# A hand-ordered two-stage chunk pipeline for a linear-attention and spectral-filter kernel

What was changed: the per-chunk attention output is formed in its natural layout and then transposed, the bonus term is summed on VectorE in place of TensorE, the key product moves to GpSimd, the inverse transform is done at half length, all small PSUM tiles share one ring of six buffers, and the order of all instructions is written by hand in place of the automatic one.

## Chip, cores and metric

One core of one Trainium2 chip. The metric is device microseconds of one execution of the program. The engines are named as the profile names them: PE (TensorE, matmul), PEld (its weight load), DVE (VectorE), ACT (ScalarE), POOL (GpSimd), SP (SyncE, which only issues DMA transfers here). With one core only the time itself can tell a slow execution. Executions of the same kernel differ by 1 to 2%, so I quote medians and, where there is one, the ratio with its 95% interval.

The device time of an execution is a little longer than the span of its profile: the profiled run of the kernel before took 224.11 us on the device with a span of 222.3 us. All the positions in a trace below are in the span's time.

## The reference

Batch 4, 8 heads, 768 steps, head size 48, model width 384. Stage 1 is a recurrent attention with a per-step decay, stage 2 a long convolution by FFT between two gates.

```python
def _attn_ref(r, k, v, w, u):                # all [4, 8, 768, 48], u [8, 48]
    state = zeros((B, H, D, D))
    for t in range(S):
        cur = einsum('bhd,bhe->bhde', u[None] * kt, vt)      # the bonus term
        y[:, :, t] = einsum('bhd,bhde->bhe', rt, state + cur)
        state = wt[..., None] * state + einsum('bhd,bhe->bhde', kt, vt)
    return y

def _moe_ref(x, w_proj, filter_fft, w_out):  # x = y as [4, 768, 384]
    proj = x @ w_proj
    x1, x2, x3 = ...                         # three slices of 384 columns
    X2 = rfft(x2, axis=1);  H = rfft(filter_fft, axis=0)
    x2_conv = irfft(X2 * H, n=S, axis=1)
    return (x1 * x2_conv * x3) @ w_out
```

## The kernel before

The recurrence is done in chunks of 128 steps, 24 chunks in all (4 batches of 6). A chunk needs the cumulated decay (two matmuls against triangular masks), exponentials of it, keys and queries scaled by them, scores masked to the past, and a carried state. When a batch's six chunks are done, its [384 x 768] transposed output `xT` feeds stage 2: projections, sums and differences of halves, a forward transform by matmul, spectral products on DVE, an inverse transform by matmul, a gate multiply, the output projection. Stage 2 of one batch is filled in between the chunks of the next. The parts that matter here:

```python
    psA = ctx.enter_context(tc.tile_pool(name="psA", bufs=3, space=PSUM))
    psS = ... bufs=1;  psT = ... bufs=1;  psB = ... bufs=2      # 8 banks in four pools
    ...
    def part_a(idx):
        ...
        nc.gpsimd.tensor_copy(out=v_heads(v_bufs[idx % NV]), in_=lv)
        nc.gpsimd.tensor_mul(rk[:, :, 0:D], rb[:, :, 0:D], lk)          # r*k, for the bonus
        nc.vector.tensor_mul(kh[:, :, 0:D], lk, csi)                    # scaled key, on DVE
        ...
    def part_b(idx):
        for x, o in ((kh, 0), (rk, HP)):                                # 8 transposes on PE
            for j in range(HP):
                nc.tensor.transpose(tk[:, o + j, :], x[:, 2 * j:2 * j + 2, :], ident)
        nc.scalar.activation(out=tkT, in_=tk, func=AF.Copy)             # 128 x 1024
        ...
        for j in range(HP):                                             # bonus: 4 matmuls
            nc.tensor.matmul(kv[:, C + 2 * j:C + 2 * j + 2], tkT[:, HP + j, :], u_sb[:, j, :], ...)
        ...                                                             # scores sc, mask mt
        nc.vector.tensor_copy(out=cc, in_=kv[:, C:])
        nc.gpsimd.tensor_mul(vc, v_heads(vb), cc.to_broadcast([L, H, D]))
        ...                                                             # state
    def part_c(idx, xT):        # output straight in transposed layout: 19 matmuls of 128 columns
        for cb in range(CB):
            ...
            for n, (lh, rh) in enumerate(ops):
                nc.tensor.matmul(yT[:, cb, :], lh, rh, ...)
        nc.scalar.activation(out=xT[:, :, ci * L:(ci + 1) * L], in_=yT, func=AF.Copy)
    ...
        def prods():            # six DVE instructions over 3 x 384 columns, bf16
            nc.vector.tensor_mul(ua, xr, HR);  nc.vector.tensor_mul(ub, xi, HI)
            nc.vector.tensor_sub(pr, ua, ub)
            nc.vector.tensor_mul(ua, xr, HI);  nc.vector.tensor_mul(ub, xi, HG)
            nc.vector.tensor_add(pi, ua, ub)

        def inv(cb, hf):        # six of these per batch: 6 matmuls of 384 columns each
            for n, q in enumerate((0, 2, 4, 1, 3, 5)):
                m = m2n[:, q - 2, :] if (hf and q >= 2) else m2[:, q, :]
                nc.tensor.matmul(ps, z(f"P{q % 2}")[:, q // 2, cb * L:(cb + 1) * L], m, ...)
            nc.vector.tensor_mul(z("y")[:, cb, sl], ps, z("g")[:, cb, sl])
    ...
    for idx in range(len(chunks) + 1):      # automatic order over this program
        part_a(idx); load_weights(idx); issue_loads(idx + 3)
        fill(3)                             # three waiting pieces of stage 2
        part_c(idx - 1, ...)
        fill(3)
        part_b(idx)
        fill(3)
```

## Time and profile before

Median 222.61 us of three runs (221.51 to 223.82) at the time of the prediction; 223.22 us of four beside the kernel after.

| profiled run, span 222.3 us | PE | DVE | ACT | POOL |
|---|---|---|---|---|
| busy, whole span (us) | 181.1 | 143.8 | 124.1 | 81.6 |
| busy in one batch period of 46.4 us | 41.6 | 32.3 | 28.2 | 18.1 |

The view by stretches gives one whole batch period, from one batch's first spectral product to the next. Columns: stretch and length, then busy time with the count of instructions for PE, PEld, DVE, ACT and POOL, then the granted clock, the DMA share and GB/s.

```profile
66.90:113.28 46.38, 41.57 (x438) 28.80 (x436) 32.32 (x54) 28.22 (x55) 18.06 (x27) 1.00 0.65 134
```

PE is busy 41.57 of 46.38 us at full clock.

The groups of DVE instructions by shape show something else that the argument needs. Columns: line, engine, operation, output and inputs, shapes, count, then busy us and mean ns of one, then idle time before.

```profile
L456 DVE TENSOR_TENSOR sd_1437<-xT_841 128x384 bf16<-128x384 bf16 x3 | 3.4, 1127 | 1.7 <-ACT xT_841 L403 1.7
...
L456 DVE TENSOR_TENSOR sd_2907<-xT_2325 128x384 bf16<-128x384 bf16 x3 | 1.6, 521 | 2.7 <-ACT xT_2325 L403 2.7
L477 DVE TENSOR_TENSOR U_1007<-X_906,HI 128x1152 bf16<-128x1152 bf16 x1 | 1.4, 1440 | 0.0
...
L457 DVE TENSOR_TENSOR sd_1439<-xT_841 128x384 bf16<-128x384 bf16 x3 | 1.0, 346 | 0.0
...
L477 DVE TENSOR_TENSOR U_3119<-X_3083,HI 128x1152 bf16<-128x1152 bf16 x1 | 0.7, 749 | 0.0
```

The same instruction, bf16 from SBUF to SBUF, has two prices. The sum of two xT slices (L456) takes 1,127 ns in mid-kernel and 521 ns in the last batch (358, 847 and 359 ns; at the last of them POOL has run out of work); and the product at L477 1,440 ns and, with POOL idle, 749 ns. The difference of the same slices (L457), which follows each sum, takes 346 ns. The six products of a batch together take 5.5 us in mid-kernel (0.76 + 1.09 + 0.76 + 1.44 + 0.75 + 0.74, from the same view) and 4.5 us in the last batch.

### The profile page before, as it was taken

The numbers are of one execution on the slowest core, as the hardware profiler recorded it, in microseconds if no ns is written. First come the engines' busy times: TensorE is split into PE (matmuls) and PEld (weight loads), VectorE is DVE, ScalarE is ACT, GpSimd is POOL, SyncE is SP. The second block draws the span as 40 slices with busy tenths as digits, with TensorE's granted clock in tenths as the row PEclk, the third lists the DMA queues.
The fourth block names the chain that finished last, engine by engine and source line by source line (L and its number), as shares of the span: only waits on it lengthen the run. The fifth ranks groups of instructions, "written<-read, shape, count | busy, mean of one in ns | idle before, by whom it ended". The sixth has DMA issues, their size and how long they took to land.

```text
span 222.3 us, 4668 instructions
## 1 busy us (share of the span) xinstructions
PE 181.1 (81%) x1778; PEld 123.3 (55%) x1778; DVE 143.8 (65%) x260; ACT 124.1 (56%) x233; POOL 81.6 (37%) x129
## 2 busy tenths in 40 slices
PE   0066797988798999978898999887979999779882
PEld 0054555766555657666465666665656666645341
DVE  8946366387759845776679384786696537734730
ACT  2396447467676346576773445767842475656022
POOL 8740366447312433463423235363232432400000
PEclk9999559699999999999999999999999999999998
DMA  6999999939598244995950709987401041000022
GB/s 132 175 307 229 282 166 193 182 66 198 108 192 158 56 85 100 257 179 112 174 108 2 143 19 278 173 170 137 79 3 35 0 147 69 4 0 0 3 106 108
DMA packets 105863, 27.44 MB, mean 123 GB/s; under 512 B 100464, under 2 KB 105456, under 8 KB 105840
## 3 DMA queue, kind: packets, MB, share of 16 engines
q1 hardware_dynamic: 105040, 25.96, 54.7%
q0 software_dynamic: 800, 1.18, 3.1%
q8 instruction: 14, 0.23, 0.5%
q14 instruction: 9, 0.07, 0.1%
HBM read 23.59 MB, written 4.72 MB: 127 GB/s over the span
## 4 chain that ended last, share of the span: by engine, by line
PE 53%; DVE 20%; ACT 12%; DMA 6%; issue 6%; SPq 1%; POOL 1%; DVEq 0%; ACTq 0%; POOLq 0%
PE yT L400 10%; PE ps_p L431 9%; PE ps_i L485 9%; DMA r_84<-in_r_dram 5%; PE ps_o L495 4%; DVE mt L362 4%; PE ps_f L254 3%; PE rT L317 3%; PE ps_f L246 3%; PE sc L355 3%; DVE g L443 2%; ACT tkT L337 2%; DVE sd_1437 L456 2%; DVE sd_2179 L456 2%; DVE sd_695 L456 2%
## 5 line engine op out<-in xcount | busy, mean ns | idle before, releaser
L362 DVE TENSOR_TENSOR mt<-sc,mask_excl 128x1024 bf16<-128x1024 f32 x24 | 29.2, 1216 | 1.1 <-PE sc L355 1.1
L337 ACT ACTIVATE tkT<-tk 128x1024 bf16<-128x1024 bf16 x24 | 24.6, 1023 | 1.4 <-PE tk L335 1.2
L490 DVE TENSOR_TENSOR y<-ps_i,g 128x384 bf16<-128x384 f32 x24 | 12.8, 555 | 16.5 <-PE ps_i L485 16.5
L431 PEld LDWEIGHTS <-wproj 128*128 128x128 bf16 x144 | 13.4, 99 | 14.1 <-issue 6.9
L499 ACT ACTIVATE o<-ps_o 128x384 f32<-128x384 f32 x24 | 11.4, 493 | 15.8 <-PE ps_o L495 15.8
L318 ACT ACTIVATE csi<-csi 128x384 f32<-128x384 f32 x24 | 11.6, 482 | 13.8 <-PE csi L310 13.8
L360 DVE COPY cc<-kv 128x8 f32<-128x8 f32 x24 | 3.9, 164 | 23.0 <-PE kv L347 22.8
L400 PE MATMUL yT<-ident,vc 128*128 128x128 bf16 x72 | 16.2, 225 | 2.2 <-POOL vc L364 2.2
L495 PE MATMUL ps_o<-wout,y 128*128 128x384 bf16 x72 | 15.2, 326 | 1.3 <-DVE y L490 0.7
L364 POOL TENSOR_TENSOR vc<-v_87,cc 128x384 bf16<-128x384 bf16 x8 | 6.6, 830 | 16.3 <-DVE cc L360 16.2
L272 PE MATMUL m2t<-ident,F 128*128 128x128 bf16 x18 | 2.8, 305 | 11.5 <-DVE ident L190 11.5
L324 DVE TENSOR_TENSOR qT<-rT,e_96 128x512 bf16<-128x512 f32 x12 | 8.2, 687 | 5.0 <-ACT e_96 L319 5.0
L355 PE MATMUL sc<-qT,tkT 48*128 48x128 bf16 x192 | 11.3, 223 | 0.0
L321 POOL TENSOR_TENSOR rk_93<-r_84,ld_k 128x384 bf16<-128x384 f32 x6 | 6.0, 999 | 13.1 <-PE tk L335 7.0
L400 PE MATMUL yT<-qT,st_98 128*128 128x128 bf16 x72 | 9.9, 219 | 0.7 <-DVE kh_91 L322 0.6
L368 POOL TENSOR_TENSOR phi<-e_95,blk 128x8 f32<-128x8 f32 x12 | 2.9, 244 | 20.4 <-ACT e_95 L319 17.3
L495 PEld LDWEIGHTS <-y 128*128 128x128 bf16 x72 | 6.6, 97 | 6.7 <-DVE y L490 1.9
L254 PE MATMUL ps_f<-ab,F 128*128 128x384 bf16 x48 | 9.7, 327 | 0.2
L400 PE MATMUL yT<-mt,v_87 128*128 128x128 bf16 x80 | 8.9, 219 | 1.1 <-DVE mt L362 1.1
L364 POOL TENSOR_TENSOR vc<-v_86,cc 128x384 bf16<-128x384 bf16 x8 | 6.6, 831 | 8.2 <-DVE cc L360 8.2
L400 PE MATMUL yT<-mt,v_88 128*128 128x128 bf16 x80 | 8.7, 225 | 0.8 <-DVE mt L362 0.8
L324 DVE TENSOR_TENSOR qT<-rT,e_95 128x512 bf16<-128x512 f32 x12 | 8.2, 684 | 1.4 <-ACT e_95 L319 1.2
(278 smaller groups left out, 538.4 us busy)
## 6 DMA issues: line engine op xcount, KB each, us to landing
ld_w<-in_w_dram SPq DMA_DIRECT2D x24, 192.0 KB, 3.9
ld_k<-in_k_dram SPq DMA_DIRECT2D x24, 192.0 KB, 3.2
ld_v<-in_v_dram SPq DMA_DIRECT2D x24, 192.0 KB, 4.2
out_dram<-o SPq DMA_DIRECT2D x3, 1152.0 KB, 5.2
filt<-in_moe_filter_fft_dram SPq DMA_DIRECT2D x2, 1152.0 KB, 8.2
r_82<-in_r_dram SPq DMA_DIRECT2D x6, 192.0 KB, 4.0
r_83<-in_r_dram SPq DMA_DIRECT2D x6, 192.0 KB, 3.6
r_84<-in_r_dram SPq DMA_DIRECT2D x6, 192.0 KB, 4.0
```

The lines of the kernel that those rows point to most:

```text
L254: nc.tensor.matmul(ps, F[:, ti, c0:c0 + L], x[:, ti, :], start=(ti == 0), stop=(ti == NT - 1),)
L324: nc.vector.tensor_mul(qT, rT, e[:, :, 0:L])
L337: nc.scalar.activation(out=tkT, in_=tk, func=AF.Copy)
L355: nc.tensor.matmul(sc[:, par, j, :], tkT[p0:p0 + D, j, :], qT[p0:p0 + D, j, :], start=True, stop=True,)
L362: nc.vector.tensor_mul(mt, sc.rearrange("p q j t -> p (q j) t"), _mid(mask_excl, H))
L364: nc.gpsimd.tensor_mul(vc, v_heads(vb), cc.to_broadcast([L, H, D]))
L400: nc.tensor.matmul(yT[:, cb, :], lh, rh, start=(n == 0), stop=(n == len(ops) - 1))
L431: nc.tensor.matmul(ps, wproj[:, cb, col0:col0 + L], xT[:, cb, sl], start=(cb == 0), stop=(cb == CB - 1),)
L456: nc.vector.tensor_add(z(f"sd{0}")[:, :, sl], lo, hi)
L485: nc.tensor.matmul(ps, z(f"P{q % 2}")[:, q // 2, cb * L:(cb + 1) * L], m, start=(n == 0), stop=(n == 5),)
L490: nc.vector.tensor_mul(z("y")[:, cb, sl], ps, z("g")[:, cb, sl])
L495: nc.tensor.matmul(ps, z("y")[:, cb, ti * L:(ti + 1) * L], wout[:, cb, :], start=(cb == 0), stop=(cb == CB - 1),)
```

## The change

Its intent is to take work from PE and to fill the idle POOL, and to let a batch period shrink from PE's pace to one that all engines share. The core of the diff, with cuts:

```diff
-    psA = ctx.enter_context(tc.tile_pool(name="psA", bufs=3, space=PSUM))
+    psA = ctx.enter_context(tc.tile_pool(name="psA", bufs=6, space=PSUM))
-    psT = ...
-    psB = ...
[...]
+    u_bc = consts.tile([L, H, D], FP32)          # u on all partitions
[...]
+    def bonus_a(idx):
+        nc.gpsimd.tensor_mul(rk, r_bufs[idx % NR][:, :, 0:D], t["lk"])
+        nc.gpsimd.tensor_mul(t["rku"], rk, u_bc)
+        nc.gpsimd.tensor_copy(out=t["vb"], in_=t["lv"])
+    def bonus_b(idx):
+        nc.vector.tensor_reduce(out=cc, in_=t["rku"], axis=AX.X, op=ALU.add)
+        nc.gpsimd.tensor_mul(t["vc"], t["vb"], cc.to_broadcast([L, H, D]))
[...]
-        nc.vector.tensor_mul(kh[:, :, 0:D], lk, csi)
+        nc.scalar.activation(out=en, in_=csi, func=AF.Exp, scale=-1.0)
+        nc.gpsimd.tensor_mul(kh[:, :, 0:D], t["lk"], en)
[...]
-        for x, o in ((kh, 0), (rk, HP)):
-            for j in range(HP):
-                nc.tensor.transpose(tk[:, o + j, :], x[:, 2 * j:2 * j + 2, :], ident)
+        for j in range(HP):
+            nc.tensor.transpose(tk[:, j, :], kh[:, 2 * j:2 * j + 2, :], ident)
[...]
+            nxt = s1.tile([L, HP, 2, D], BF16, tag="S", name="S")      # state: added on PE,
+            nc.vector.tensor_mul(nxt, kv, t["phi"].to_broadcast(...))   # scaled on DVE
[...]
-    def part_c(idx, xT):          # 19 matmuls of 128 columns, transposed layout
+    def output(idx):              # natural layout: 1 of 384, 4 of 96, 8 of 48 columns
+        nc.tensor.matmul(y, ident, t["vc"], start=True, stop=False)
+        ... 4 x qT against S; 8 x mt against vb
+        nc.scalar.activation(out=xn, in_=y, func=AF.Copy)
+    def turn_x(idx, xT):          # three transposes and a second eviction
+        for cb in range(CB):
+            nc.tensor.transpose(yt[:, cb, :], t["xn"][:, cb * L:(cb + 1) * L], ident)
+        nc.scalar.activation(out=xT[:, :, ci * L:(ci + 1) * L], in_=yt, func=AF.Copy)
[...]
-        def inv(cb, hf):
-            ... 6 matmuls of 128 rows and one multiply, six times a batch
+        def inv(cb):              # even and odd part, three times a batch
+            ... 4 matmuls of 128 rows, 4 of 64 rows in pairs
+            nc.scalar.activation(out=ods, in_=od, func=AF.Copy)
+            nc.vector.tensor_add(eo[:, 0, :], ev, ods)
+            nc.vector.tensor_sub(eo[:, 1, :], ev, ods)
+            nc.vector.tensor_mul(z("y")[:, cb, :], eo..., z("g")[:, cb, :])   # 768 columns
[...]
+    with tc.manual_schedule(engines={ENG.PE, ENG.Activation, ENG.DVE, ENG.Pool, ENG.SP}):
+        begin(0); decay(0); bonus_a(0); begin(1); bonus_b(0); bonus_a(1)
+        for idx in range(len(chunks)):
+            turn(idx); begin(idx + 2); load_weights(idx); issue_loads(idx + 4)
+            fill(2)                                  # FILL = (2, 2, 2, 0)
+            scores(idx); decay(idx + 1); bonus_b(idx + 1); bonus_a(idx + 2)
+            fill(2)
+            output(idx)
+            fill(2)
+            turn_x(idx, xTs[b])
```

Filler for the first chunks is the setup of stage 2: six turns of the transform matrix, then six transforms of the filter.

## The prediction

> **What bounds the kernel now.** In the chain in order of time, batch b's first spectral product starts at 66.90, 113.28 and 159.61 us: 46.35 us per batch, 67 us before the first, 19.6 us after the last (202.7 to 222.3). In one period (busy time by stretch) PE is busy 41.6 us, DVE 32.3, ACT 28.2, POOL 18.1, DMA share 0.65. PE's busy time includes latency: by the spacing of starts, a 384-column matmul takes 0.163 us, a 128-column one 0.055. Estimate from counts: stage 1 takes 2.96 us of PE per chunk (19 output matmuls, 8 key and bonus transposes, 4 bonus matmuls), stage 2 126 x 0.163 = 20.5 us, together 38.4 of 46.35. The other 8 us are waits of PE's in-order queue; the chain's shares are PE 53%, DVE 20%, ACT 12%.
>
> **The change, per batch** (estimates from those durations).
> - PE: natural-layout output, no bonus transposes or matmuls: 2.96 to about 2.4 us per chunk, -3.3. Half-length inverse: 36 to 18 equivalents, if its 64-row matmuls run in pairs as the score matmuls do in this trace (8 in 0.40 us): -2.9. About 32 remain. The Trainium skill, "TensorEngine Tiling (Array Packing)", Tiling Modes, says that row tiles execute in parallel.
> - DVE: loses kh (6 x 0.55), cc (6 x 0.16) and 6 y multiplies (0.555); gains a reduce (6 x about 0.5), add and sub of the inverse (6 x 0.55), three gate multiplies (0.5 to 1.0). About 33.
> - POOL: gains kh and the u product (about 1 us each per chunk), loses the state multiply: 18 to 26. "SBUF — State Buffer", Who interferes with whom, says that a DVE instruction with two SBUF inputs contends with a GpSimd one that reads SBUF. The trace agrees: the sum of two xT slices took 1.13 us in mid-kernel, 0.36 at the end with POOL idle. More POOL work lengthens sums, products and gate multiply: DVE 34.
> - ACT: the key turn drops from 1.02 to about 0.59; one more eviction per chunk (0.49), three per batch: 30.
> - Six-deep PSUM ring, hand order, fill of 6 units per chunk against 36 per batch: fewer order stalls.
>
> The bound moves from PE with latency to DVE (34), PE (32), ACT (30) and DMA (0.65 x 46 = 30), nearly level. Coupled in-order engines won't reach 100%; I take 88%: 38.5 us per batch.
>
> **Ends.** The first batch's last transposed output ends at 59.6 us now; I expect 49.5 (start of work at 13 us stays, chunks become shorter). The tail after the last such output (197.35) is 25 us now; products will overlap the transforms and the inverse is shorter, but all three inverse blocks must finish before the first output matmul: 20 us. Sum: 49.5 + 3 x 38.5 + 20 = 185.
>
> **Predicted: 185 us, 174 to 203. Chances: faster 0.93, same 0.04, slower 0.03.**
>
> **Right if:** the period is 37 to 40.5 us; PE busy falls by 20 us or more in total; DVE becomes the busiest engine (over 80%) and holds much of the chain; POOL is near 65%; 64-row inverse matmuls start in pairs; sums and products lengthen; the tail is near 20 us.
>
> **Wrong if:** the fixed order lines up badly (PE standing at each score mask, 1.22 us, or at the output's eviction and turn) and the period stays above 42; the key product, slower on POOL, lies on the chunk chain; DMA starts to limit; output matmuls of 48 columns cost as much as those of 128; or POOL costs DVE more than 2 us per batch. Better than 174 if a chunk runs at PE's rate.

## More of the kernel before

The next lines are from the page of the kernel before: first the busy time of each engine, then rows of the view in 40 slices, where each digit is the busy share of one slice of 5.6 us in tenths, and PEclk is the granted clock of PE in tenths.

```profile
PE 181.1 (81%) x1778; PEld 123.3 (55%) x1778; DVE 143.8 (65%) x260; ACT 124.1 (56%) x233; POOL 81.6 (37%) x129
...
PE   0066797988798999978898999887979999779882
...
DVE  8946366387759845776679384786696537734730
...
POOL 8740366447312433463423235363232432400000
PEclk9999559699999999999999999999999999999998
```

PE is near 9 for most of the span, POOL near 4.

## The result

The kernel after took 204.53 us (median of four, 202.64 to 205.64) beside 223.22 us, ratio 0.9165 with a 95% interval of 0.9074 to 0.9256: faster. A ratio here is always the mean time of one kernel's fast runs over that of the other's of the same rounds, so it is not quite the ratio of the medians. Executions over 1.5% slower than the fastest of the same kernel are left out of the means. The time lies just above the predicted range of 174 to 203 us, and 19.5 us above the predicted 185.

The page of the kernel after, the same rows as before:

```profile
PE 155.5 (76%) x1490; PEld 97.3 (48%) x1490; DVE 154.4 (76%) x249; ACT 127.3 (63%) x269; POOL 119.6 (59%) x162
...
PE   0176097796889679779999397799993978998762
...
DVE  8343364789577997999669999996699999729750
...
POOL 5089516796968927468978564879796538100000
PEclk9999559999699957999999979999999799999789
```

PE's busy time fell by 25.6 us (181.1 to 155.5). DVE's rose from 143.8 to 154.4 us and POOL's from 81.6 to 119.6. The PE row shows a 0 in the fifth slice (20 to 25 us). Later it has a low digit (6, 3 and 3 in slices 14, 23 and 31) once in each batch, and PEclk falls in the slice that follows it. PEclk also has a 6 in slice 11, late in the first batch.

To see where the time went I cut the span at the ends of the last eviction of `xT` of each batch, as the prediction did.

| us | before | predicted | after | missed by |
|---|---|---|---|---|
| until the first batch's xT is complete | 59.6 | 49.5 | 56.3 | 6.8 |
| three batch periods | 137.8 | 115.5 | 123.8 | 8.3 |
| after the last xT | 25.0 | 20 | 23.6 | 3.6 |
| span | 222.3 | 185 | 203.7 | 18.7 |

The profiled execution of the kernel after is the slowest of its four (205.64 us; the fastest took 202.64), so up to 3 us of these misses belong to this one execution. All three terms missed on the same side. The first one has its main cause in one place of the chain of waits. Here the chain in order of time (start us, length us, what), up to the first filter transform:

```profile
15.03 0.83 SPq L93
15.90 7.95 DMA filt<-in_moe_filter_fft_dram
23.88 1.37 DVE fs L232
25.29 2.08 PE ps_f L223 x6
```

SP is busy issuing loads until 15.90 us, then the filter's own load lands 7.95 us later, DVE forms the sum of its halves, and only then can PE start. The list of waits (engine, line, what it waited for, us in total, times, longest) says what it cost PE:

```profile
PE ps_f L223 <- DVE fs L232: 6.1, 1, 6.1
```

PE stood 6.1 us with the second chunk's work behind the transform in its queue; the second chunk took 15.0 us from xT to xT where the third took 4.25. A smaller part is the clock. It was at half from 51.4 to 54.8 us, and the sixth chunk took 6.46 us; in the profiled executions of e2, e3 and e9 below, which have the same order in the start and no half clock at that point, it took 4.94 to 4.95 us.

A period, chunk by chunk, in batch 2. Columns as in the view by stretches before; each stretch runs from one xT eviction to the next.

```profile
103.15:108.54 5.39, 5.39 (x66) 3.77 (x67) 3.92 (x6) 5.01 (x12) 4.86 (x7) 1.00 0.95 175
108.54:119.61 11.07, 7.36 (x65) 4.16 (x63) 10.93 (x14) 4.22 (x9) 7.30 (x8) 0.85 1.00 177
119.61:126.64 7.03, 5.95 (x68) 3.76 (x67) 6.58 (x10) 4.34 (x9) 3.68 (x5) 1.00 0.32 61
126.64:133.92 7.28, 6.18 (x66) 3.88 (x64) 7.25 (x12) 4.61 (x11) 4.85 (x7) 1.00 0.51 91
133.92:139.19 5.27, 5.18 (x57) 3.51 (x56) 3.84 (x6) 5.17 (x14) 4.86 (x7) 1.00 0.42 91
139.19:144.55 5.36, 5.27 (x57) 3.40 (x57) 4.53 (x6) 5.30 (x14) 3.94 (x7) 1.00 1.09 286
sum 41.40, PE 35.33 PEld 22.48 DVE 37.04 ACT 28.64 POOL 29.49; mean PE 5.89 PEld 3.75 DVE 6.17 ACT 4.77 POOL 4.92
```

Three chunks (11.07, 7.03, 7.28 us, 25.4 together) have DVE busy for 24.8 us of it; the other three (16.0 us) are filled by PE and ACT, both 15 to 16. So a period of 41.4 us has no single limit: the three chunks that hold the products and the gates run at DVE's pace, the others at PE's and ACT's. DVE sums to 37.04 us, 89% of the period. The worst is the chunk of 11.07 us, and in it PE's clock was 0.85. That chunk of batch 1 on DVE, in order of time (start us, length us, what):

```profile
65.31 0.75 DVE L455 TENSOR_TENSOR U_1077<-X_956,HR 128x1152 bf16<-128x1152 bf16 x1
65.98 1.38 DVE L456 TENSOR_TENSOR U_1078<-X_962,HI 128x1152 bf16<-128x1152 bf16 x1
67.39 1.45 DVE L457 TENSOR_TENSOR P_1075<-U_1077,U_1078 128x1152 bf16<-128x1152 bf16 x1
68.87 1.36 DVE L458 TENSOR_TENSOR U_1077<-X_956,HI 128x1152 bf16<-128x1152 bf16 x1
70.15 1.05 DVE L459 TENSOR_TENSOR U_1078<-X_962,HG 128x1152 bf16<-128x1152 bf16 x1
71.24 1.43 DVE L460 TENSOR_TENSOR P_1076<-U_1077,U_1078 128x1152 bf16<-128x1152 bf16 x1
72.59 1.01 DVE L427 TENSOR_TENSOR g<-ps_p,x_622 128x384 bf16<-128x384 f32 x2
73.53 1.21 DVE L343 TENSOR_TENSOR mt<-sc,mask_excl 128x1024 bf16<-128x1024 f32 x1
```

The six products now take 7.42 us (0.75 + 1.38 + 1.45 + 1.36 + 1.05 + 1.43), against 5.5 us before and 4.5 undisturbed. They are one block: the gates and the chunk's own score mask `mt` wait behind it. PE at the same time:

```profile
69.22 0.32 PE L467 MATMUL ps_e<-m_171,P_1075 128*128 128x384 bf16 x1
72.73 0.50 PE L467 MATMUL ps_e<-m_171,P_1076 128*128 128x384 bf16 x1 [3.19 <-DVE P_1076 L460]
```

The bracket is idle time and its releaser: PE issued the first inverse matmul at 69.22, then stood 3.19 us for the second product, with the next chunk's work behind in its order. And the clock in single microseconds of the same stretch (columns as above):

```profile
71.00:72.00 1.00, 0.00 (x0) 0.00 (x0) 0.97 (x2) 0.00 (x0) 1.00 (x1) 0.94 0.00 0
72.00:73.00 1.00, 0.27 (x1) 0.13 (x2) 1.00 (x2) 0.00 (x0) 0.73 (x2) 0.50 0.00 0
...
78.00:79.00 1.00, 1.00 (x8) 0.56 (x5) 1.00 (x2) 1.00 (x3) 0.92 (x2) 0.64 0.00 0
```

PE ran at half clock from about 71.9 us, 0.8 us before the stand ended, to about 78.7 us (the microseconds between, not shown, all have 0.50): about 6.8 us, worked out from the shares 0.94 and 0.64 of the first and last. In batches 2 and 3 PE stood 3.18 us at the same place, and the half clock lasted only 3.4 us each time, beginning after the stand had ended (116.3 to 119.7 and 157.2 to 160.6 us). The Trainium skill, "TensorE: Matmul & The Clock Gate", Part 1 with its "HAM oscillation", describes this: a monitor of the array's activity halves its clock after an idle window of about 3.4 us, and "The abstract rule is 'no PE-idle gaps >~3.4µs.'" This trace agrees in kind (a stand, then 0.50), but its stands of 3.19 and 3.18 us are a little shorter than that.

The groups on DVE that grew or came new (columns as for the groups before):

```profile
L483 DVE TENSOR_TENSOR y<-eo,g 128x768 bf16<-128x768 bf16 x12 | 14.0, 1164 | 0.4
L290 DVE TENSOR_REDUCE cc<-rku 128x8 f32<-128x384 bf16 x24 | 13.0, 541 | 1.8 <-POOL rku L281 1.8
...
L436 DVE TENSOR_TENSOR sd_1353<-xT_866 128x384 bf16<-128x384 bf16 x3 | 2.9, 957 | 0.0
...
L435 DVE TENSOR_TENSOR sd_1351<-xT_866 128x384 bf16<-128x384 bf16 x3 | 1.6, 522 | 2.0 <-ACT xT_866 L385 2.0
```

The gate multiply of 768 columns takes 1,164 ns in the mean of twelve; the nine in mid-kernel take 1.37 us in the mean and the three at the very end, with POOL idle, 0.56 us. Of the sums and differences of xT, the differences (L436) grew from 346 to 957 ns, but the sums (L435) shrank from 1,127 to 522 ns: in the batch shown these six instructions took 4.4 us before and 4.4 us after, and only which of them is hit has changed (5.0 and 5.8 us in the first batch, 4.4 and 4.7 in the third). The new reduction takes 541 ns, nearly the same everywhere (536 to 553). "SBUF — State Buffer", Who interferes with whom, in the Trainium skill, states both: a DVE instruction with two SBUF inputs contends with a GpSimd one that reads SBUF, whoever comes first blocking the other, and a reduction never contends. This trace agrees in the pattern, and POOL's own multiplies lengthen too (the product of r and k ranges from 1.00 to 1.51 us in batch 2). The score mask `mt`, which reads the scores from PSUM, kept its length (1,216 ns before, 1,211 after).

### The profile page after: what moved, and what is told of

Its sections match the earlier page's. It is cut to its first block, busy times and chain, and to the rows that moved or that the text cites. A ratio compares the mean times of both kernels' runs of the same rounds, so it can differ in the third digit from the quotient of the medians.

```text
span 203.7 us, 4170 instructions
## 1 busy us (share of the span) xinstructions
PE 155.5 (76%) x1490; PEld 97.3 (48%) x1490; DVE 154.4 (76%) x249; ACT 127.3 (63%) x269; POOL 119.6 (59%) x162
## 4 chain that ended last, share of the span: by engine, by line
PE 33%; DVE 25%; ACT 19%; issue 9%; SPq 7%; DMA 4%; POOL 0%; ACTq 0%; DVEq 0%
PE ps_p L415 8%; DVE mt L343 5%; DMA filt<-in_moe_filter_fft_dram 4%; ACT tkT L326 4%; PE yn L371 3%; ACT o L494 3%; PE sc L338 3%; ACT xn L376 3%; ACT ab L445 3%; PE rT L307 2%; SPq L91 2%; DVE g L427 2%; PE ps_o L490 2%; SPq L93 2%; SPq L90 2%
## 5 line engine op out<-in xcount | busy, mean ns | idle before, releaser
L291 POOL TENSOR_TENSOR vc<-v,cc 128x384 bf16<-128x384 bf16 x24 | 20.9, 872 | 34.9 <-PE yt L384 16.5
L343 DVE TENSOR_TENSOR mt<-sc,mask_excl 128x1024 bf16<-128x1024 f32 x24 | 29.1, 1211 | 9.3 <-PE sc L338 9.3
L281 POOL TENSOR_TENSOR rku<-rk,u_bc 128x384 bf16<-128x384 bf16 x24 | 24.4, 1017 | 1.9
L312 POOL TENSOR_TENSOR kh_83<-ld_k,en 128x384 bf16<-128x384 f32 x12 | 12.0, 999 | 16.1 <-ACT en L310 16.0
L376 ACT ACTIVATE xn<-yn 128x384 bf16<-128x384 f32 x24 | 11.8, 490 | 15.2 <-PE yn L371 14.5
L310 ACT ACTIVATE en<-csi 128x384 f32<-128x384 f32 x24 | 11.9, 496 | 9.7 <-PE csi L301 9.3
L312 POOL TENSOR_TENSOR kh_84<-ld_k,en 128x384 bf16<-128x384 f32 x12 | 13.8, 1148 | 2.6 <-ACT en L310 2.6
L326 ACT ACTIVATE tkT<-tk 128x512 bf16<-128x512 bf16 x24 | 14.4, 598 | 0.8 <-PE tk L324 0.8
L282 POOL CAST v<-ld_v 128x384 bf16<-128x384 f32 x24 | 14.5, 605 | 0.0
L290 DVE TENSOR_REDUCE cc<-rku 128x8 f32<-128x384 bf16 x24 | 13.0, 541 | 1.8 <-POOL rku L281 1.8
L483 DVE TENSOR_TENSOR y<-eo,g 128x768 bf16<-128x768 bf16 x12 | 14.0, 1164 | 0.4
L338 PEld LDWEIGHTS <-tkT 48*128 48x128 bf16 x192 | 5.9, 97 | 11.2 <-ACT tkT L326 10.2
L355 DVE TENSOR_TENSOR S<-kv,phi 128x384 bf16<-128x384 f32 x20 | 10.9, 544 | 0.0
```

Of the source, the lines that this page charges most:

```text
L281: nc.gpsimd.tensor_mul(t["rku"], rk, u_bc)
L282: nc.gpsimd.tensor_copy(out=t["vb"], in_=t["lv"])
L291: nc.gpsimd.tensor_mul(t["vc"], t["vb"], cc.to_broadcast([L, H, D]))
L312: nc.gpsimd.tensor_mul(kh[:, :, 0:D], t["lk"], en)
L338: nc.tensor.matmul(sc[:, par, j, :], tkT[p0:p0 + D, j, :], qT[p0:p0 + D, j, :], start=True, stop=True,)
L343: nc.vector.tensor_mul(mt, sc.rearrange("p q j t -> p (q j) t"), _mid(mask_excl, H))
```

## The experiments

Every kernel below is the kernel after with one thing changed, or a stated combination of such changes. Medians of four executions each, and the three terms of the table above from the profiled one:

| run | changed against the kernel after | median us | ratio to before (95%) | first / periods / tail |
|---|---|---|---|---|
| after | | 204.53 | 0.9165 (0.9074–0.9256) | 56.3 / 123.8 / 23.6 |
| e1_setup_late | no filler in the second chunk | 199.37 | 0.8939 (0.8886–0.8992) | 49.1 / 122.5 / 25.0 |
| e2_full_inverse | old inverse | 199.50 | 0.8933 (0.8886–0.8979) | 54.9 / 120.9 / 22.1 |
| e3_weave | products in thirds | 215.44 | 0.9639 (0.9572–0.9705) | 53.4 / 135.5 / 22.7 |
| e4_pool_light | two POOL products left out, wrong result | 191.17 | 0.8536 (0.8472–0.8600) | 52.3 / 113.0 / 24.6 |
| e5_tile_order | automatic order | 205.22 | none | 62.9 / 115.6 / 23.8 |
| e7_late_full | e1 + e2 | 195.51 | 0.8764 (0.8701–0.8827) | 51.7 / 119.9 / 22.1 |
| e8_late_full_two | e7, products in two groups | 201.73 | 0.9022 (0.8941–0.9102) | 51.0 / 126.9 / 22.1 |
| e9_warm | idle matmuls before the inverse | 202.06 | 0.9039 (0.8966–0.9112) | 54.4 / 121.4 / 22.8 |
| e10_hand_start | e1, automatic order from the fourth chunk on | 196.78 | 0.8830 (0.8783–0.8877) | 54.7 / 119.1 / 22.7 |
| e11_hand_start_full | e10 + e2 | 202.53 | 0.9039 (0.8967–0.9110) | 56.0 / 121.9 / 20.5 |
| e12_singles | e7, products one by one | 197.89 | none | 51.8 / 121.2 / 22.1 |
| e13_old_bonus | bonus on PE again | 200.47 | 0.8976 (0.8930–0.9022) | 56.4 / 117.7 / 25.1 |
| e14_late_bonus | e1 + e13 | 193.45 | 0.8697 (0.8626–0.8769) | 50.5 / 117.7 / 22.9 |
| e15_late_bonus_dve | e14, bonus turn evicted by DVE | 213.08 | none | 55.6 / 132.6 / 23.9 |
| e16_late_bonus_full | e14 + e2 | 196.22 | 0.8834 (0.8765–0.8903) | 51.5 / 120.8 / 22.0 |
| e17_late_bonus_dve_full | e16, bonus turn evicted by DVE | 207.57 | 0.9301 (0.9236–0.9365) | 54.1 / 129.6 / 22.0 |

Where "none" stands, too few of the executions counted as fast for a ratio. The medians are of all four executions, slow ones too: one each of e4, e8, e11 and e13 counted as slow, two of e5 and e12, three of e15. All results were right except e4's.

### e1_setup_late: is the start lost to the filter's load?

```diff
             issue_loads(idx + 4)
+            FILL = (0, 0, 0, 0) if idx == 1 else (2, 2, 2, 0)
             fill(FILL[0])
```

> No filler work in the second chunk, so that the six filter transforms come one chunk later. Theory S (the start): in the changed kernel PE's in-order queue stood 6.1 us at the first filter transform, for a filter that landed at 23.8 us, behind the loads of four chunks; without that stand the last chunk of the first batch ends 5 to 6 us sooner (55.8 to about 50 us) and the whole is about 199 us. Rival: the start is limited by the loads themselves (DMA share 1.0 from 11 to 40 us), then the waits only move and the gain is under 2 us (203 us or more).

Measured: 199.37 us. The first batch's xT is complete at 49.1 us, against 56.3 and a predicted 49.5; PE waits 0.9 us for the filter's sum in place of 6.1, by the list of waits of this run:

```profile
PE ps_f L223 <- DVE fs L232: 0.9, 1, 0.9
```

The second chunk came down from 15.0 to 4.2 us, the third now takes 9.8 with the transforms. The periods hardly move (122.5 against 123.8). The tail grew by 1.4 us; there the 16 output matmuls took 4.44 us in place of 2.77, because they ran at half clock. So this stand is most of the start's miss of 6.8 us, and 5.2 us reach the total. About 1.5 us of the 7.2 by which the profiled starts differ are not the edit's: they are the half clock at 51.4 us in the kernel after, which this execution does not have.

### e2_full_inverse: is the half-length inverse a gain at all?

```diff
-            ev, od = ps2("ps_e"), ps2("ps_o")
-            ... (even and odd parts, eviction, add, sub, one multiply of 768 columns)
+            for hf in (0, 1):
+                ps = ps2("ps_i")
+                for n, q in enumerate((0, 2, 4, 1, 3, 5)):
+                    m = m2n[:, q - 2, :] if (hf and q >= 2) else m2[:, q, :]
+                    nc.tensor.matmul(ps, z(f"P{q % 2}")[:, q // 2, col], m, ...)
+                sl = halves[hf]
+                nc.vector.tensor_mul(z("y")[:, cb, sl], ps, z("g")[:, cb, sl])
```

> The old full-length inverse (both halves by 12 matmuls per block, gate straight from PSUM) in the new order. Theory D: in three of the six chunks of each batch DVE is full (24.8 of 25.4 us), and the half-length inverse put 7.4 us per batch on DVE (add, sub, gate multiply of 1.34 us) where the old one has 3.3; so undoing it, though it gives PE back 2.9 us per batch, takes 3 to 4 us off each period: about 192 us, DVE busy about 16 us less. Theory P: PE and its waits bound the kernel; then PE's extra 2.9 us per batch make it slower, 208 to 214 us.

Measured: 199.50 us, 5 us faster than the kernel after: the direction of the theory that DVE's time sets the period, at two fifths of the expected size (5.0 of 12.5 us). DVE's busy time fell from 154.4 to 146.6 us; the chunk that holds the inverse and outputs fell from 7.28 to 5.67 us. By the groups of DVE, the add, sub and gate multiply of the half-length inverse take 27.2 us in all four batches (6.6 + 6.6 + 14.0), the multiplies from PSUM in their place 12.8 us. Of this gain 3.1 us return in the setup, as sign-turned copies of the matrices, and 1.7 us in longer sums of xT, so the saving is smaller than counted. What PE saves by the half length is not what the period waits for. The tail is 1.5 us shorter in this profile, but that is not the inverse alone: here the clock stayed at 1.00 through the tail, and in the kernel after it was at half for 3.4 us. Three runs with the half-length inverse and full clock in the tail (e3, e9, e14) had tails of 22.7, 22.8 and 22.9 us. By these the inverse is worth about 0.7 us there and the half clock about 0.8.

### e3_weave: the last batch's finer order for all batches

```diff
-        if b < B - 1:
+        if False:      # all batches: transforms in pairs, products in thirds between them
             ready[5] += fws + [F(prods, slice(0, 3))]
```

> Every batch takes the order of the last one: products in three pieces woven between transforms and gates, in place of one block of six instructions. Theory P: the block of 7.3 us on DVE made PE stand 3.2 us once per batch and then run about 6 us at half clock; weaving removes that stand, the granted clock rises from 0.92 to 0.97 or more, and each of three periods loses 3 us or more: 195 us or less. Theory D: DVE is full there whatever the order, and the three pieces cost it about 1 to 2 us more per batch (0.36 us for a third against 0.75 for the whole, where not disturbed); then 203 to 209 us, even if the clock rises.

Measured: 215.44 us, 11 us slower, so neither theory had the size. The products' chunk grew from 11 to 14.2 us. PE stood twice in it, up to 2.3 us each for L457 and L460, in place of once for 3.2; a third of a product took 0.63 us in the mean in mid-kernel against 0.36 in the tail, and DVE's busy time rose to 160.6 us. The 18 pieces of a batch took DVE 11.3 us in mid-kernel, where the six whole products take 7.4, and the last third still came just before the inverse that needs it. The clock stayed at 0.925.

### e4_pool_light: what does POOL's extra work cost DVE?

Its output is wrong, which doesn't matter for the time. The bonus sum is taken of `v`. It removes two of POOL's multiplies per chunk and leaves every DVE instruction in place.

```diff
-        nc.gpsimd.tensor_mul(rk, r_bufs[idx % NR][:, :, 0:D], t["lk"])
-        nc.gpsimd.tensor_mul(t["rku"], rk, u_bc)
-        nc.vector.tensor_reduce(out=cc, in_=t["rku"], axis=AX.X, op=ALU.add)
+        nc.vector.tensor_reduce(out=cc, in_=t["vb"], axis=AX.X, op=ALU.add)
```

> Wrong result on purpose: POOL makes neither r*k nor r*k*u, DVE reduces v in their place, so POOL's work per batch falls from 29.7 to about 17 us and DVE has the same instructions. Theory C (contention): DVE's instructions with two SBUF inputs are stretched by POOL (products 7.4 us per batch, gate multiply 1.34 us, against 4.5 and 0.57 when POOL is idle); they shorten by about 40% of that excess, 3 us per batch, DVE busy falls by 9 us or more in all and the time to about 196 us. Without contention as a cause, DVE's instructions keep their lengths and the time stays within 2 us of 204.

Measured: 191.17 us (the three fast executions 189.21 to 191.56), 13 us faster. POOL's busy time fell from 119.6 to 69.9 us and DVE's from 154.4 to 138.1 with the same 249 instructions. DVE groups of this run, same columns:

```profile
L479 DVE TENSOR_TENSOR y<-eo,g 128x768 bf16<-128x768 bf16 x12 | 10.2, 847 | 0.4
...
L432 DVE TENSOR_TENSOR sd<-xT 128x384 bf16<-128x384 bf16 x12 | 5.1, 424 | 0.0
...
L453 DVE TENSOR_TENSOR P<-U,U 128x1152 bf16<-128x1152 bf16 x3 | 2.8, 940 | 0.1
```

The gate multiply fell from 1,164 to 847 ns in the mean of twelve, the difference of two xT slices from 832 (the mean of three times 957 to 960 and 450) to 424, the first spectral difference (L457 of the kernel after) from 1,442 to 940, and the six products of a batch from 7.4 to 6.0 us. The profiled execution is one that counted as slow by time, but its granted clock (0.96) is that of two of the fast ones. This shows that about 16 us of DVE's time were the company of these two POOL instructions per chunk. A rival reading is that the total fell because POOL's own queue became shorter. It does not fit the trace of the kernel after: from the first complete xT (56.3 us) to the end, the only wait for POOL in its list is one of 0.4 us, by ACT.

### e5_tile_order: what is the hand order worth?

```diff
-    with tc.manual_schedule(engines={ENG.PE, ENG.Activation, ENG.DVE, ENG.Pool, ENG.SP}):
+    if True:
```

> The changed kernel without the hand order: the same operations, issued in the order that the automatic scheduler makes of them, as in the kernel before. It prices the hand order alone. Theory H: the hand order and the fixed fill are most of the gain (the kernel before lost 8 of 46 us per batch to waits of PE): about 218 us. Theory W: the gain is the work taken from PE, whatever the order: within 3 us of 204.5.

Measured: 205.22 us (202.61 to 206.89; the two fast executions 202.61 and 204.43), not to be told apart from the kernel after (202.64 to 205.64). The two differ in where they lose: the automatic order completes the first xT at 62.9 us (PE stood 13.2 us for a key product that POOL had queued behind the r·k of a later load), but its periods are 40.4, 39.9 and 35.2 us. So the hand order gains 6.6 us at the start and gives it back in the periods. As no ratio could be formed, a difference of 1 or 2 us in the total stays open.

### e7_late_full: do e1 and e2 add?

The two edits together.

> Both mends together: no filler work in the second chunk, and the full-length inverse. If the two gains lie in different stretches (the start; the DVE-full chunks and the tail) they add: 204.5 - 5.2 - 5.0 = about 194 us. If the start's gain is partly given back later, 197.

Measured: 195.51 us, 9.0 us faster than the kernel after; 5.2 + 5.0 would be 10.2. They nearly add, as was expected if one acts at the start and the other in periods and tail.

### e8_late_full_two: products in two groups

e7 with the first three products (real part) before the gates and the last three between them.

```diff
-            ready[5] += fws + [F(prods, slice(0, 3))]
-            ready[5] += g1[0:4] + invs[0:1] + g1[4:6] + invs[1:3]
+            ready[5] += fws + [F(prods, slice(0, 3), 0)] + g1[0:4]
+            ready[5] += [F(prods, slice(0, 3), 1)] + g1[4:6] + invs
```

> As the run with both mends, and the six product instructions of a batch in two groups of three with four units of filler work between them, at full width, so that no instruction is added. Theory L (lumping): of the six chunks of a batch three are full on DVE and three have 0.5 to 1.5 us of room there; half the products move into a chunk with room and each period loses 1 to 1.5 us: about 190 us. Theory P (PE's stand): the stand before the inverse, 3.2 us, goes as well, and the period loses 3 us: 185 us. If the first result of the thirds holds for any split (11 us slower than the block), 200 or more.

Measured: 201.73 us, 6 us slower than e7. The theory that the length of one block was the trouble fails: PE now stood up to 3.9 us for the last product, and the products' chunk took 12.0 to 12.8 us in place of 9.9 to 11.3.

### e9_warm: how much of it is the half clock?

Eighteen matmuls whose result nobody reads, placed before the first inverse, to fill the stand.

```diff
+        def warm():
+            ps = ps2("ps_w")
+            for _ in range(18):
+                nc.tensor.matmul(ps, wproj[:, 0, 0:L], wproj[:, 0, 0:C], start=True, stop=True)
...
-            ready[5] += g1[0:4] + invs[0:1] + g1[4:6] + invs[1:3]
+            ready[5] += g1[0:4] + [F(warm)] + invs[0:1] + g1[4:6] + invs[1:3]
```

> The changed kernel with 18 idle matmuls (384 columns, about 2.9 us) in front of the first inverse of batches 0 to 2, where PE otherwise stands 3.2 us. The result stays right. Theory K (clock): the stand makes the granted clock fall to half for about 6 us, and that costs 2 us per batch; without the stand the clock of that chunk goes from 0.85 to near 1.0 and the time to about 198 us. Theory D: DVE is full in that chunk (10.9 of 11.1 us), so the clock rises and the time stays within 1.5 us of 204.5.

Measured: 202.06 us. The stretch of 66 to 79 us, first in the kernel after:

```profile
66.00:79.00 13.00, 9.81 (x75) 5.45 (x73) 12.86 (x16) 5.57 (x13) 9.15 (x9) 0.74 0.65 121
```

and in this one:

```profile
66.00:79.00 13.00, 11.98 (x108) 6.83 (x104) 12.86 (x17) 5.77 (x12) 9.15 (x11) 1.00 0.51 91
```

The clock of the stretch rose from 0.74 to 1.00. DVE's busy time there is 12.86 us in both, and it filled both. The periods fell by 1.4, 0.6 and 0.4 us, in all 2.4, in step with the half clock that they had before (6.8, 3.4 and 3.4 us). So in the profiled executions the half clock costs about 0.8 us per batch in the mean, and DVE's full chunk the rest. That the medians differ by 2.5 us too is partly chance: the profiled executions differ by 5.3 us (205.64, the slowest of the kernel after, and 200.33, the fastest here), and the rest lies in the start (1.9) and the tail (0.8), where the edit changes nothing and this execution happened to have less half clock. The result lies between the two theories.

### e10_hand_start and e11_hand_start_full: hand order for the start alone

e10 is e1 with the hand order for three chunks and the automatic one after; e11 has the old inverse as well.

```diff
-        for idx in range(len(chunks)):
-            ... (the body of the loop)
+        for idx in range(3):
+            chunk(idx)
+    for idx in range(3, len(chunks)):          # outside the hand order
+        chunk(idx)
```

> Hand order for the first three chunks only (with no filler work in the second), the automatic order from there on. The run with automatic order throughout was even with the hand order in all (205 us), and its profile says why: its start is 6.6 us later (PE stood 13 us for a key product that POOL's queue held behind a multiply of a later load), its three periods are shorter (40.4, 39.9 and 35.2 us against 42.0, 41.3 and 40.4). If both readings hold, the two good parts add: first batch ends at 49 to 50 us, periods near 38.5, tail 24: about 189 us. If the shorter periods were the flattery of the late start, 197 to 199, as the hand order with the mended start.

> The same, with the full-length inverse. In the hand order that inverse was worth 4 to 5 us because three chunks of a batch were full on DVE. If the automatic order is still limited by DVE it is worth as much again: about 185 us. If the automatic order has moved the limit to PE, where the full-length inverse costs 2.9 us per batch, 190 to 196.

Measured: 196.78 and 202.53 us (200.12 to 202.86 in e11's three fast executions). e10 is 2.6 us faster than e1, with a last period of 36.3 us but a start that lost 5.6 us of e1's. e11 is about 5.5 us slower than e10: under the automatic order the old inverse loses what it gained by hand. The better mixture (e10) is not below the better hand order (e7, 195.51).

### e12_singles: one product between every two gates

```diff
-            ready[5] += fws + [F(prods, slice(0, 3))]
-            ready[5] += g1[0:4] + invs[0:1] + g1[4:6] + invs[1:3]
+            ready[5] += fws
+            for n in range(6):
+                ready[5] += [F(prods, slice(0, 3), n), g1[n]]
+            ready[5] += invs
```

> Hand order with both mends (195.5 us), and the six product instructions of a batch issued one by one at full width, one filler unit between each two, and all gates in front of the inverse. Theory Q (queue): the block of products holds the next chunk's score mask on DVE for 5.5 us, and with it ACT (idle 6.9 us) and PE; the split into two groups failed only because the second group stood right in front of the inverse. Singly issued, the mask waits for two instructions at most (2.5 us), and the period loses 2 us or more: 189 us or less. Rival: the products' time on DVE has to be spent in those chunks whatever the grain, and the later inverse gives PE a new stand: 195 to 201 us.

Measured on the basis of e7: 197.89 us (195.98 to 199.16; no ratio). Two of the four counted as slow; the fast ones, 195.98 and 196.77 us, stand beside 195.05 to 196.10 of e7. So splitting does not pay at this grain either, and whether it costs anything cannot be told. Three grains were tried (thirds, two groups, singles), and none gained; PE still waited 2.6 us per batch for the last product.

### e13_old_bonus: the bonus back on PE

This takes the second POOL product and the reduction away again, with a right result: r·k is transposed with the key, four small matmuls sum it, and DVE only copies the 8 columns.

```diff
-        nc.gpsimd.tensor_mul(t["rku"], rk, u_bc)
-        nc.vector.tensor_reduce(out=cc, in_=t["rku"], axis=AX.X, op=ALU.add)
+        for j in range(HP):
+            nc.tensor.transpose(tk[:, HP + j, :], rk_bufs[idx % 3][:, 2 * j:2 * j + 2, :], ident)
+        for j in range(HP):
+            nc.tensor.matmul(ccp[:, 2 * j:2 * j + 2], t["tkT"][:, HP + j, :], u_sb[:, j, :], ...)
+        nc.vector.tensor_copy(out=cc, in_=ccp)
```

> The changed kernel with the bonus summed on PE again (transposes of r*k, matmuls with u, the double-width eviction), one part of the change undone. It takes r*k*u from POOL (1 us per chunk) and the reduce from DVE (0.54 us, for a copy of 0.16), and gives PE about 0.45 and ACT 0.43 us per chunk. By theory D the three DVE-full chunks gain 0.4 to 0.7 us each and the three that are full on ACT and PE lose 0.45 each: within 3 us of 204.5. If PE or ACT bounds all chunks, 3 us per period are lost: 213 us. If POOL's contention is the chief cost everywhere, 199 us or less.

Measured: 200.47 us (200.04 to 200.87 in the three fast executions), 4.1 us faster than the kernel after. DVE's busy time fell by 27.5 us to 126.9, POOL's by 30.9 to 88.7; PE's rose by 5.8 and ACT's by 11.6 (the key turn is 1,024 columns again). The same DVE groups as in e4:

```profile
L490 DVE TENSOR_TENSOR y<-eo,g 128x768 bf16<-128x768 bf16 x12 | 7.9, 657 | 0.4
...
L443 DVE TENSOR_TENSOR sd<-xT 128x384 bf16<-128x384 bf16 x12 | 4.2, 349 | 0.0
...
L464 DVE TENSOR_TENSOR P<-U,U 128x1152 bf16<-128x1152 bf16 x3 | 2.8, 941 | 0.1
```

The gate multiply is at 657 ns, the differences at 349, and the six products sum to 5.5 us again. The chunk of the products fell from 11.1 to 7.9 us. The light chunks rose from 5.3 to 5.9 us, where ACT is busy 5.4 to 5.8 of it. So the period falls from 41.3 to 39.2 us in the mean: part of the gain on DVE is paid to ACT. The tail grew by 1.5 us; in this execution it has two stretches of half clock (184.2 to 187.7 and 191.1 to 194.5 us). This run undoes two things at once, the reduction on DVE and the multiply on POOL; with e4, which kept the reduction, it says that the contention is a good part of it and not how large the rest is.

### e14_late_bonus: the two settled causes together

e1 and e13 together.

> Bonus on PE again, and no filler work in the second chunk; the rest as changed. If the two effects add: 204.5 - 5.2 - 4.0 = about 195 us, first batch ended at 49 to 51 us, periods 38 to 39, tail 25.

Measured: 193.45 us, ratio 0.8697 to before, the fastest with a right result. It beats both kernels: 29 us below before and 11 us below the change as made. Its page:

```profile
PE 155.1 (81%) x1682; PEld 103.7 (54%) x1682; DVE 128.3 (67%) x254; ACT 138.5 (73%) x269; POOL 91.2 (48%) x138
```

PE is the fullest engine again at 81%, then ACT, DVE and POOL; the mean clock was 0.99, where the kernel after had 0.925. Its terms are 50.5 + 117.7 + 22.9 us against the predicted 49.5 + 115.5 + 20. In the profiled execution the products' chunk took 7.9 us in two batches and 9.5 us in one, which had a clock of 0.82 in that chunk.

### e15_late_bonus_dve and e17_late_bonus_dve_full: relieve ACT of the longer turn

e14 (and e16) with the bonus half of the turn evicted by DVE, as ACT was the new limit of the light chunks. The edit also moves the bonus sum behind the score mask.

```diff
-        nc.scalar.activation(out=tkT, in_=tk, func=AF.Copy)            # 1024 columns
+        nc.scalar.activation(out=tkT, in_=tk[:, 0:HP, :], func=AF.Copy)
+        nc.vector.tensor_copy(out=rkT, in_=tr)
```

> As the run before it, and the second half of the eviction (the transposed r*k, 512 columns) moves from ACT to DVE, with the bonus sum behind the score mask. With the bonus on PE, ACT was busy 31.5 us per period and full (5.75 of 5.9 us) in the chunks without products, DVE only 28.8. If ACT is the limit there, those three chunks go from 5.9 to about 5.4 us and the whole to about 190 us. If PE is (36 us busy, latency included), no change: 194 to 196.

> All of it: bonus on PE with half its eviction on DVE, full-length inverse, no filler work in the second chunk. If the limits are ACT in the light chunks and DVE in the heavy ones, both are relieved: 188 us or less. If PE has become the limit, 194 to 198 us.

Measured: 213.08 us (no ratio; three of four slow, the profiled one too, the fast one 208.95) and 207.57 us. Both failed. The periods grew to 44 and 42 to 44 us: PE's bonus matmuls now waited for a DVE eviction (13.3 us of waits at the weight load in e15) that stands in DVE's queue behind products, gates and sums of xT. Less work on the fuller engine did not help; what the trace shows in its place is this new dependence on DVE in the chunks. The later place of the bonus sum may have a part in it, and no run tells the two apart.

### e16_late_bonus_full: does the old inverse still gain?

e14 with the edit of e2.

> Bonus on PE, no filler work in the second chunk, and the full-length inverse. That inverse was worth 4 to 5 us while DVE was full. With DVE no longer full (127 of 199 us) its 2.9 us more of PE per batch should count: if PE is the next limit, slower than the same with the half-length inverse by 3 us or more (198). If DVE is still the limit in the chunks with products and gates, faster by 2 to 4 us (191 to 193).

Measured: 196.22 us, 2.8 us slower than e14, where the same edit had gained 5.0 us on the kernel after. The sign turned. DVE's busy time fell here too (128.3 to 123.7 us), but DVE was no longer the limit; PE's rose from 155.1 to 162.1 and the periods from 117.7 to 120.8 us. This fits the reading that in the kernel after the half-length inverse loses by its DVE time.

## Why the prediction was right or wrong

**Right.** The mechanism on PE: its busy time fell by 25.6 us ("20 us or more"), and by 6.2 us per batch (41.57 to 35.33), which is the sum of the predicted 3.3 and 2.9. The 64-row inverse matmuls start in pairs; in the tail of the kernel after (start us, length us, what):

```profile
189.08 0.34 PE L467 MATMUL ps_o<-m_171,P_3021 128*128 128x384 bf16 x1 [1.36 <-DVE P_3021 L457]
190.14 0.34 PE L467 MATMUL ps_o<-m_171,P_3022 128*128 128x384 bf16 x1 [0.72 <-DVE P_3022 L460]
190.41 0.33 PE L474 MATMUL ps_e<-m_171,P_3021 64*128 64x384 bf16 x1
190.41 0.33 PE L474 MATMUL ps_o<-m_171,P_3021 64*128 64x384 bf16 x1
```

Two of them start at 190.41 together, as the Trainium skill's "TensorEngine Tiling (Array Packing)", Tiling Modes, says of row tiles. The key turn on ACT takes 0.598 us (predicted 0.59). The products and the gate multiply lengthen, as said; the sums of xT do not (1,127 to 522 ns, while the differences lengthen). DVE's use of the period was 89%, predicted 88%; but the 88% was taken without a derivation, so that it fits is partly luck. POOL's load rose as expected in kind, to 29.5 us per period rather than 26.

**Wrong: "More POOL work lengthens sums, products and gate multiply: DVE 34", and with it "38.5 us per batch".** This is the step that failed: the mechanism was right, but DVE's term of the sum was mis-sized. It allowed 1 us for it (33 to 34); DVE measured 37.0 us per batch. At the prediction's own 88% that would be 42.1 us per batch; 41.3 was measured. The prediction itself named the danger, "POOL costs DVE more than 2 us per batch", and that came true. The products take 7.4 us per batch in place of 5.5, and the gate multiply three times 1.37 us in mid-kernel, where 0.5 to 1.0 was allowed: +1.9 and, against the middle of that range, +1.9 us per batch. e4 shows that POOL's instructions are the cause: without two of them per chunk 249 DVE instructions of the same shapes took 16.3 us less and the total 13 us less. e13 shows it with a right result. The half-length inverse belongs in the same term: with its gate multiply, which is counted above, it costs DVE 3.6 us per batch (27.2 less 12.8, by four), where the prediction's figures give 2.2 (3.3 and three times 0.75, less six times 0.555), in exchange for PE work that the period was not waiting for (undoing it gains 5.0 us in e2; where DVE is relieved first, undoing it loses 2.8 us in e16).

**Wrong by omission: the half clock.** The prediction assumed PE at full clock. The block of products holds PE for 3.2 us just before the inverse in each batch, and the clock is then at half for 6.8 us in batch 1 and for 3.4 us in batches 2 and 3. By the profiled execution of e9 this costs 1.4, 0.6 and 0.4 us, 2.4 in the three periods. Two more stretches of 3.4 us, in the first batch and in the tail, cost about 1.5 and 0.8 us of the profiled execution; the profiled executions of e2, e3 and e9 have neither.

**Wrong: "The first batch's last transposed output ends at 59.6 us now; I expect 49.5".** It ended at 56.3. The step assumed that filling the first chunks with the setup costs nothing; it put a transform that needs the filter's late load into PE's fixed order. e1 moves it by one chunk and gets 49.1 us, so the size of this step was about right and one wait was overlooked (its share is about 5.3 of the 6.8 us, the rest is the half clock at 51.4 us). An automatic order does not heal it: e5 stood elsewhere, 13.2 us.

**Wrong: "20 us" for the tail.** It measured 23.6 us. Of the 3.6 us about 0.7 are the half-length inverse and about 0.8 the half clock (by the tails of e2, e3, e9 and e14, see e2). The rest I can only describe: PE stands 1.36 and 0.72 us for the last products and the clock falls to 0.50 from about 191.4 to 194.8 us, over most of the inverse. No run tried the stands alone, so about 2 us of the tail stay open.

**Also wrong:** "DVE over 80%" and "POOL near 65%" of the whole span; they were 76% and 59%, as the longer start and tail have less of either. And the prediction gave the fixed order some worth in "fewer order stalls"; e5 shows none in the total.

The 18.7 us of the table are thus mostly settled: about 5.3 at the start (e1), 2.4 of the clock in the periods (e9) and about 2.3 in start and tail, the DVE term in the periods (e2, e4, e13), 0.7 of the inverse in the tail. These effects overlap, so I do not sum them. What stays open is about 2 us of the tail, and why splitting the products never paid: in e3, e8 and e12 PE still waited 2.1 to 3.9 us for a product just before the inverse, which fits a last product that comes no earlier, but no run moved that product far ahead.

## What to carry to other kernels

When work is moved to an idle engine, price what the move does to the neighbours that share its ports: here 50 us less of GpSimd work made the same count of vector instructions 16 us shorter. A cheaper form on one engine is worth nothing unless that engine sets the pace, and its sign can turn when another part of the change is undone, so test the parts in both settings. In a hand-written order, look first for the one instruction that waits for a late load with everything else queued behind it.

## What the Trainium skill lacked or had wrong

- "TensorE: Matmul & The Clock Gate", Part 1, gives the rule "no PE-idle gaps >~3.4µs". Here stands of 3.19, 3.18 and 3.18 us were already followed by half clock, and so were two stands of 1.36 and 0.72 us in the tail, with one matmul of 0.34 us between them (0.50 from about 191.4 to 194.8 us). So gaps shorter than the rule names are not safe, and the page gives no lengths for short idle times. A rule of the busy share alone does not come out of this trace either: PE was busy for 1.55 us of the 3.41 us before that drop; but 1.93 us of the 3.42 us from 47.99 us on were followed by half clock too, and 1.58 us of the 3.41 us from 194.77 us on by full clock.
- "SBUF — State Buffer", Who interferes with whom, says who blocks whom, but gives no price for a mix of instructions. Here it was: six products 4.5 us with POOL idle, 5.5 with POOL at 37% of the span, 7.4 with POOL at 59%; the 768-column gate multiply 0.56 us alone, 1.37 in the mix; the 384-column multiply on POOL itself 1.00 to 1.51 us.
